# Split products for seven of the eight experts, and the narrowing of a second layer's weights dealt out anew

## The chip, the cores and the metric

The kernel runs on one core of a Trainium2 chip. TensorE is PE here (its weight loads are PEld), VectorE is DVE, ScalarE is ACT, GpSimd is POOL; SP only issues transfers. The metric is the device time of one execution in microseconds, as the median of several runs; less is better.

## The reference, cut to what matters

```python
def reference(...):
    x = attention(q, k, v)            # 2304 tokens of 512 features, unchanged here
    # first layer: 8 experts, 288 tokens each, chosen by a greedy assignment on x @ w_gate
    for e in range(8):
        h = np.maximum(x[assigned == e] @ w1[e], 0.0)      # 512 -> 1024
        out[assigned == e] = h @ w2[e]                     # 1024 -> 512
    # second layer, one weight pair for all tokens
    h = out @ w_in                                         # 512 -> 2048
    sp = np.where(h > 20.0, h, np.log1p(np.exp(np.minimum(h, 20.0))))
    return (h * np.tanh(sp)) @ w_out                       # 2048 -> 512
```

All of it is to be computed to float32 accuracy. The weights `w_in` and `w_out` reach the kernel as 64-bit floats.

## The kernel before, in words

Up to about 205 us the kernel computes the attention and the first routing rounds. Then three things run interleaved:

- **Routing**, one round per expert (`Router.phase`, written R0 to R7). A round picks the next expert and its 288 tokens by a digit search: seven levels, each a comparison on DVE (`cmp`, L353), 18 small counting products on PE (`cnt`, L411), a reduction on DVE (`jk`, L415), a small product (`j`, L417), and two more DVE operations. At its end POOL gathers the token rows (`xrow`, L615), and `r.last` marks the DVE operation that gives their indices.
- **Experts**, E0 to E7 in the order list and one to eight in this text. An expert transposes its rows on PE (`xtp`, L630), copies them to `xh`, and goes through eight slices of 128 hidden features: four products for the hidden slice `hp` (L661), a Relu on ACT (`hh`, L662), and two slices later four products into the output `ya` (L638). All are plain float32 products; PE runs each as two records. The weights come by SP in blocks of 128x512, `w1` from a pool of six buffers and `w2` from one of eight. The output of 288 tokens is split on ACT and DVE into a rounded part `Yh` and a rest `Yl`, which stand in a ring of 512 columns and are stored to `y_dram`.
- **Narrowing**, 32 pieces (`Narrow.steps`): a 128x512 block of 64-bit weights is turned into a rounded float32 and a rest in `wM_sb`. A piece is a load by SP of 0.5 MB into one of two raw buffers, one or two ACT operations, four or five DVE operations with integer bit work, two or three POOL operations and one more on ACT. Its first operation (`hold`) stands behind `r.last`.

The second layer follows in two passes over nine groups of 256 tokens: G for hidden features 0 to 1023, whose results go to `part`, and P for the rest. A group loads `Yh` and `Yl` back from `y_dram` into the ring (POOL's queue, L677), and takes four steps of two slices. A step is 24 split products into `hm` (`mm3`, L597 to L599: rounded by rounded, rounded by rest, rest by rounded, three records of 256 columns each), a chain of five ACT and five DVE operations that gives `gh` and `gl`, and, three steps later, 12 records of 512 columns into `oa`. The G pass needs pieces 0 to 15, the P pass 16 to 31; the latter stand in memory that the experts' pools give back.

The order list says how many pieces follow each expert or group: `E0/2` deals a piece to each of the first two of its eight slices. The order of instructions on each engine is then made by the scheduler of the framework out of this program; every engine takes its instructions strictly in that order.

## Time and profile before

| | |
|---|---|
| median of 2 runs | 1007.25 us (1007.13 to 1007.38) |
| the profiled execution | 1006.99 us, span 1005.2 us |
| PE busy | 918.9 us, 91% of the span, mean clock 0.943 |
| DVE busy | 605.3 us, 60% |
| ACT busy | 435.9 us, 43% |
| POOL busy | 265.2 us, 26% |
| moved by DMA | 123.45 MB, mean 123 GB/s |

The span runs from the first to the last instruction of that execution; the rest of its time lies outside. Busy time of PE is that of records whose ends are modelled, so a full PE says that nothing else was waited for, and the spacing of starts says what one record costs. A bracket behind a timeline row holds the idle time of the engine before it and what ended it. The granted clock is 1.00 at 2.4 GHz and about half at the lower level.

### The profile page before, as it was taken

What the parts mean: (1) busy time and instruction counts of PE and PEld (TensorE: products, weight loads), DVE (VectorE), ACT (ScalarE), POOL (GpSimd) and SP (SyncE); (2) the same over time, 40 slices, a digit from 0 to 9 for tenths busy, and PEclk for the clock granted to TensorE, in tenths of its full rate; (3) what the DMA queues carried; (4) which work ended last, traced back from release to release, by engine and by line L of the source; (5) the groups of instructions that cost most, each with busy time, mean ns of one, the idle gap of its engine ahead of it and who ended that gap; (6) DMA issues with size and microseconds to landing.
All of it is one profiled execution on the core that took longest, in us unless ns stands there. A gap on an engine that the chain in (4) does not pass through costs nothing.

```text
span 1005.2 us, 18188 instructions
## 1 busy us (share of the span) xinstructions
PE 918.9 (91%) x6804; PEld 743.3 (74%) x6804; DVE 605.3 (60%) x1633; ACT 435.9 (43%) x1097; POOL 265.2 (26%) x294
## 2 busy tenths in 40 slices
PE   5999996399999999999977489799999999999995
PEld 3778775267676676767756488688999899999994
DVE  5798885545646454654511599975555565665654
ACT  4577672002121211212321376566565656555553
POOL 5444310204133140406611545530000011111101
PEclk8799997589999999999979689899999999999998
DMA  8557412516455553536741634422222324433311
GB/s 230 150 159 201 145 59 96 150 42 201 133 170 160 166 191 106 191 112 201 252 169 38 160 102 126 126 63 64 64 63 64 84 64 127 111 98 85 84 42 63
DMA packets 76375, 123.45 MB, mean 123 GB/s; under 512 B 12192, under 2 KB 40096, under 8 KB 76288
## 3 DMA queue, kind: packets, MB, share of 16 engines
q1 hardware_dynamic: 36448, 75.10, 24.6%
q0 software_dynamic: 21984, 28.32, 11.1%
q10 hardware_dynamic: 17856, 18.88, 5.5%
q8 instruction: 54, 0.88, 0.4%
q14 instruction: 33, 0.27, 0.1%
HBM read 98.67 MB, written 23.60 MB: 122 GB/s over the span
## 4 chain that ended last, share of the span: by engine, by line
PE 45%; issue 18%; DVE 16%; ACT 10%; POOL 6%; DMA 5%; SPq 0%; POOLq 0%; DVEq 0%; ACTq 0%
PE hp L661 12%; PE ya L638 11%; PE cnt L411 4%; DVE eu L730 3%; DVE eu L729 3%; PE sp L173 3%; PE pvl L213 3%; DVE eu L732 2%; ACT eu L726 2%; ACT r L727 2%; PE trl L199 2%; DMA n<-in_wM_dram 2%; PE rp L229 2%; ACT r L728 2%; DVE gl L736 2%
## 5 line engine op out<-in xcount | busy, mean ns | idle before, releaser
L597 PE MATMUL hm<-Yh,wM_sb 128*128 128x256 f32 x576 | 166.8, 290 | 32.5 <-DMA Yh<-y_dram 16.9
L598 PE MATMUL hm<-Yl,wM_sb 128*128 128x256 f32 x576 | 165.7, 288 | 0.4 <-DMA Yl<-y_dram 0.4
L599 PE MATMUL hm<-Yh,wM_sb 128*128 128x256 f32 x576 | 165.3, 287 | 0.0
L661 PE MATMUL hp<-xh,w 128*128 128x288 f32 x512 | 151.0, 423 | 0.0
L638 PE MATMUL ya<-hh,w 128*128 128x288 f32 x512 | 149.7, 420 | 0.0
L597 PEld LDWEIGHTS hm<-Yh,wM_sb 128*128 128x128 f32 x576 | 113.5, 197 | 39.3 <-DVE eu L732 19.0
L598 PEld LDWEIGHTS hm<-Yl,wM_sb 128*128 128x128 f32 x576 | 114.0, 198 | 3.1 <-DVE nz L551 0.7
L597 PE MATMUL oa<-wM_sb,gh 128*128 128x512 f32 x288 | 113.3, 393 | 2.7 <-ACT gh L735 2.7
L599 PEld LDWEIGHTS hm<-Yh,wM_sb 128*128 128x128 f32 x576 | 113.7, 197 | 0.0
L599 PE MATMUL oa<-wM_sb,gl 128*128 128x512 f32 x288 | 113.6, 394 | 0.0
L598 PE MATMUL oa<-wM_sb,gh 128*128 128x512 f32 x288 | 113.5, 394 | 0.0
L661 PEld LDWEIGHTS hp<-xh,w 128*128 128x128 f32 x512 | 93.2, 192 | 23.5 <-issue 0.2
L729 DVE SCALAR_TENSOR_TENSOR eu<-eu,r 128x512 f32<-128x512 f32 (+1 forms) x73 | 53.4, 731 | 94.2 <-ACT r L728 94.2
L638 PEld LDWEIGHTS ya<-hh,w 128*128 128x128 f32 x512 | 91.6, 190 | 22.7 <-PE hp L661 0.2
L662 ACT ACTIVATE hh<-hp 128x288 f32<-128x288 f32 x64 | 26.0, 408 | 187.0 <-PE hp L661 172.6
L735 ACT CAST gh<-eu 128x512 fp32r<-128x512 f32 (+1 forms) x73 | 44.7, 612 | 107.4 <-DVE eu L732 107.3
L736 DVE TENSOR_TENSOR gl<-eu,gh 128x512 fp32r<-128x512 f32 (+1 forms) x73 | 55.0, 753 | 37.5 <-ACT gh L735 37.4
L726 ACT ACTIVATE eu<-eu,one_sb 128x512 f32<-128x512 f32 (+1 forms) x73 | 52.3, 717 | 42.2 <-DVE eu L725 41.5
L415 DVE TENSOR_SCALAR_CACHE_REDUCE jk<-cnt 8x64 f16<-8x64 f32 (+2 forms) x49 | 11.1, 227 | 92.3 <-PE cnt L411 92.3
L597 PEld LDWEIGHTS oa<-wM_sb,gh 128*128 128x128 f32 x288 | 54.8, 190 | 12.6 <-ACT gh L735 3.2
L599 PEld LDWEIGHTS oa<-wM_sb,gl 128*128 128x128 f32 x288 | 54.4, 189 | 11.8 <-DVE gl L736 0.4
L704 POOL DMA_INDIRECT out_dram<-osb,ixs x18 | 19.4, 1079 | 163.9 <-DVE osb L703 161.1
(151 smaller groups left out, 1697.6 us busy)
## 6 DMA issues: line engine op xcount, KB each, us to landing
w<-in_wE_dram SPq DMA_DIRECT2D x128, 256.0 KB
n<-in_wM_dram SPq DMA_DIRECT2D x32, 512.0 KB
Yh<-y_dram POOLq DMA_DIRECT2D x18, 512.0 KB
Yl<-y_dram POOLq DMA_DIRECT2D x18, 512.0 KB
vw<-in_vw_dram SPq DMA_DIRECT2D x16, 315.0 KB
kT<-in_kT_dram SPq DMA_DIRECT2D x16, 291.0 KB
qT<-in_qT_dram SPq DMA_DIRECT2D x16, 288.0 KB
vd<-in_vd_dram SPq DMA_DIRECT2D x16, 288.0 KB
```

The lines of the kernel that those rows point to most:

```text
L173: self.nc.tensor.matmul(sp[r, u], q[r, 64 * n:64 * n + 64], k[r, 64 * n:64 * n + W], start=False, stop=u == 2)
L213: self.nc.tensor.matmul(op[c, u], vw[:, 3 * g + u, c], d['aT'][:, u, c], start=True, stop=True)
L411: nc.tensor.matmul(cnt[:, 0:K], OH[:, c, :], cmp[c], start=False, stop=(c == 17))
L597: mm(out, lh, rh, start=first, stop=False)
L598: mm(out, lh, rl, start=False, stop=False)
L599: mm(out, ll, rh, start=False, stop=last)
L638: nc.tensor.matmul(acc[c], w2[:, 128 * c:128 * c + 128], hh[:, 0:288], start=j == 0, stop=j == 7)
L661: nc.tensor.matmul(hp, w1[:, 128 * dc:128 * dc + 128], xh[:, dc], start=dc == 0, stop=dc == 3)
L726: nc.scalar.activation(out=u, in_=e, func=AF.Square, bias=one)
L729: nc.vector.scalar_tensor_tensor(out=u, in0=u, scalar=1.0, in1=r, op0=ALU.add, op1=ALU.mult)
L735: nc.scalar.copy(gh[:, 0:w], e)
L736: nc.vector.tensor_tensor(out=gl[:, 0:w], in0=e, in1=gh[:, 0:w].bitcast(F32), op=ALU.subtract)
```

## The change

- Experts two to six (`w` in MODES) keep the plain first product. Their second product becomes a split one: ACT rounds the `w2` block into `wbh` (L607), DVE subtracts for the rest `wbl` (L611), DVE also makes the rest `gl` of the hidden slice (L705), and PE takes three records instead of two per product.
- Experts seven and eight (`s`) split both products. Their weights come as blocks of 128x1024 into three raw buffers; the subtractions go to POOL and DVE in turn; `xh` gets a rest `xl`. Expert one (`p`) stays plain.
- The pools change: for `w1` three buffers instead of six, for the raw `w2` three, for the split weights five and five.
- Narrowing: three pieces in each of experts one to five, one in expert six, none in seven and eight. In the G pass two pieces a group, behind its second and fourth step (`i % 2`) instead of the first two; a piece there may start behind the last `gl` of a step (`mark`) instead of `r.last`. The tile `nt` has one buffer instead of two.
- The ring has 544 columns. Every expert uses columns 256 to 543, the groups 0 to 255 and 256 to 511 in turn.

```diff
@@ -490,10 +490,13 @@
         self.out[k] = idx, exi, ii
-RING = 512
+RING, EPOS = 544, 256
 NV = 3
 LASTM = 1
-NRW, NWA, NWB, NGS = 2, 6, 8, 4
+
+MODES = 'pwwwwwss'
+PE4 = 2
+NRW, NWR, NWA, NWB, NGS = 2, 3, 3, 5, 4
 HC = 8
 LAGE, LAGM = 2, 3
 EXP20 = 485165195.40979
@@ -540,7 +543,7 @@
...
-            t = self.zp.tile([128, 512], F32, name="nt")
+            t = self.zp.tile([128, 512], F32, name="nt", bufs=1)
...
@@ -585,12 +588,28 @@
...
+        self.nsplit = 0
+        self.pooln = PE4
+        self.rawe = P("f_rawe", NWR, ctx_e)
...
         self.wb = P("f_wb", NWB, ctx_e)
...
+        self.mark = None
...
+
+    def split(self, src, pool, nm, eng=None):
+
+        nc = self.nc
+        wh = pool.tile([128, 512], F32R, name=nm + "h")
+        wl = pool.tile([128, 512], F32R, name=nm + "l")
+        nc.scalar.copy(wh, src)
+        if eng is None:
+            eng = nc.gpsimd if self.nsplit % self.pooln != self.pooln - 1 else nc.vector
+            self.nsplit += 1
+        eng.tensor_tensor(out=wl, in0=src, in1=wh.bitcast(F32), op=ALU.subtract)
+        return wh, wl
...
@@ -622,45 +641,69 @@
...
+        mode = MODES[k]
+        plain = mode != 's'
...
-        xh = self.xs.tile([128, 4, 288], F32, name="xh")
+        xh = self.xs.tile([128, 4, 288], F32 if plain else F32R, name="xh", tag="xh")
+        if not plain:
+            xl = self.xs.tile([128, 4, 288], F32R, name="xl")
...
-            (nc.vector.tensor_copy if dc % 2 else nc.scalar.copy)(xh[:, dc], t)
+            if plain:
+                (nc.vector.tensor_copy if dc % 2 else nc.scalar.copy)(xh[:, dc], t)
+            else:
+                nc.scalar.copy(xh[:, dc], t)
+                nc.vector.tensor_tensor(out=xl[:, dc], in0=t, in1=xh[:, dc].bitcast(F32), op=ALU.subtract)
...
-        def second(j, w2, hh):
+        def second(j, w2, hh, hl):
...
-                nc.tensor.matmul(acc[c], w2[:, 128 * c:128 * c + 128], hh[:, 0:288], start=j == 0, stop=j == 7)
+                s = slice(128 * c, 128 * c + 128)
+                if mode == 'p':
+                    nc.tensor.matmul(acc[c], w2[:, s], hh[:, 0:288], start=j == 0, stop=j == 7)
+                    continue
+                self.mm3(acc[c], w2[0][:, s], w2[1][:, s], hh[:, 0:288], hl[:, 0:288], j == 0, j == 7)
             if j == 7:
...
+                q = slice(EPOS, EPOS + 288)
                 for c in range(4):
-                    for s0, s1 in pieces:
-                        q = (pos + s0) % RING
-                        nc.scalar.copy(self.Yh[:, c, q:q + s1 - s0], acc[c][:, s0:s1])
-                        nc.vector.tensor_tensor(out=self.Yl[:, c, q:q + s1 - s0], in0=acc[c][:, s0:s1],
-                                                in1=self.Yh[:, c, q:q + s1 - s0].bitcast(F32), op=ALU.subtract)
-                for s0, s1 in pieces:
-                    q = (pos + s0) % RING
-                    for v, y in enumerate((self.Yh, self.Yl)):
-                        nc.scalar.dma_start(self.a['y_dram'][:, v, :, 288 * k + s0:288 * k + s1].bitcast(F32), y[:, :, q:q + s1 - s0].bitcast(F32))
+                    nc.scalar.copy(self.Yh[:, c, q], acc[c])
+                    nc.vector.tensor_tensor(out=self.Yl[:, c, q], in0=acc[c], in1=self.Yh[:, c, q].bitcast(F32), op=ALU.subtract)
+                for v, y in enumerate((self.Yh, self.Yl)):
+                    nc.scalar.dma_start(self.a['y_dram'][:, v, :, 288 * k:288 * k + 288].bitcast(F32), y[:, :, q].bitcast(F32))
...
+            hh = self.gs.tile([128, 512], F32 if mode == 'p' else F32R, name="gh", tag="gh")
+            hl = None
+            if plain:
+                w1 = self.wa.tile([128, 512], F32, name="w1", tag="wah")
+                nc.sync.dma_start(w1, src[:, 0:512])
+                if mode == 'p':
+                    w2 = self.wb.tile([128, 512], F32, name="w2", tag=("wbh", "wbl")[j % 2])
+                    nc.sync.dma_start(w2, src[:, 512:1024])
+                else:
+                    raw = self.wa.tile([128, 512], F32, name="w2r", tag="wal")
+                    nc.sync.dma_start(raw, src[:, 512:1024])
+                    w2 = self.split(raw, self.wb, "wb", nc.vector)
+                for dc in range(4):
+                    nc.tensor.matmul(hp, w1[:, 128 * dc:128 * dc + 128], xh[:, dc], start=dc == 0, stop=dc == 3)
+            else:
+                raw = self.rawe.tile([128, 1024], F32, name="wraw")
+                nc.sync.dma_start(raw, src)
+                w1 = self.split(raw[:, 0:512], self.wa, "wa")
+                w2 = self.split(raw[:, 512:1024], self.wb, "wb")
+                for dc in range(4):
+                    s = slice(128 * dc, 128 * dc + 128)
+                    self.mm3(hp, w1[0][:, s], w1[1][:, s], xh[:, dc], xl[:, dc], dc == 0, dc == 3)
             nc.scalar.activation(out=hh[:, 0:288], in_=hp, func=AF.Relu)
-            self.push(lambda j=j, w2=w2, hh=hh: second(j, w2, hh))
+            if mode != 'p':
+                hl = self.gs.tile([128, 512], F32R, name="gl")
+                nc.vector.scalar_tensor_tensor(out=hl[:, 0:288], in0=hp, scalar=0.0, in1=hh[:, 0:288].bitcast(F32), op0=ALU.max, op1=ALU.subtract)
+            self.push(lambda j=j, w2=w2, hh=hh, hl=hl: second(j, w2, hh, hl))
...
     def group(self, t0, half):
@@ -670,7 +713,7 @@
...
-        q = 128 * t0 % RING
+        q = 128 * t0 % 512
...
@@ -733,14 +776,14 @@
...
-            nc.vector.tensor_tensor(out=gl[:, 0:w], in0=e, in1=gh[:, 0:w].bitcast(F32), op=ALU.subtract)
+            self.mark = nc.vector.tensor_tensor(out=gl[:, 0:w], in0=e, in1=gh[:, 0:w].bitcast(F32), op=ALU.subtract)
             self.push(lambda f=f, m=m, gh=gh, gl=gl: second(f, m, gh, gl))
...
-ORDER = ('R0 R1 E0/2 R2 E1/2 R3 E2/2 R4 E3/2 R5 E4/2 R6 E5/2 R7 E6/2 E7/2 N G/2 G/2 G/2 G/2 G/2 G/2 G/2 G/2 G P P P P P P P P P').split()
+ORDER = ('R0 R1 E0/3 R2 E1/3 R3 E2/3 R4 E3/3 R5 E4/3 R6 E5/1 R7 E6 E7 N G G G G G G G G G P P P P P P P P P').split()
...
@@ -801,7 +844,7 @@
         nar.st = f.raw
         def hold(ins):
-            tc.add_manual_dep(ins.ins, r.last.ins.name, mybir.DependencyInfo(mybir.DependencyClass.NoSync, mybir.DependencyReason.DATA), reason="order")
+            tc.add_manual_dep(ins.ins, (f.mark or r.last).ins.name, mybir.DependencyInfo(mybir.DependencyClass.NoSync, mybir.DependencyReason.DATA), reason="order")
...
@@ -835,7 +878,7 @@
...
             for i, _ in enumerate(steps):
-                if i < pieces:
+                if i < pieces or i % 2 and st[0] == 'G':
                     nar.piece()
...
```

DVE, from the end of expert two's round to the second level of the next routing round (`nz` and `nt` are a piece's tiles, `jk`, `jb`, `E` and `cmp` the routing's). Before:

```order
L556 SCALAR_TENSOR_TENSOR nt<-n_4214,nt 128x512
L559 TENSOR_SCALAR nz<-nt 128x512
L564 SCALAR_TENSOR_TENSOR nz<-n_4214,nz 128x512
L415 TENSOR_SCALAR jk,fl<-cnt 8x128
L419 TENSOR_REDUCE jb<-j_4379 128x1
L631 COPY xh<-xtp 128x288
L424 TENSOR_SCALAR E<-G,jb 128x36
L631 COPY xh<-xtp 128x288
L353 TENSOR_TENSOR cmp<-E,rthr 128x2304
L405 SCALAR_TENSOR_TENSOR G<-E,dg_4334 128x18
```

In the change:

```order
L557 TENSOR_SCALAR nt<-nz 128x512
L559 SCALAR_TENSOR_TENSOR nt<-n_4242,nt 128x512
L611 TENSOR_TENSOR wbl<-w2r,wbh 128x512
L562 TENSOR_SCALAR nz<-nt 128x512
L705 SCALAR_TENSOR_TENSOR gl<-hp,gh 128x288
L554 TENSOR_SCALAR nz<-nz 128x512
L415 TENSOR_SCALAR jk,fl<-cnt 8x128
L419 TENSOR_REDUCE jb<-j_4506 128x1
L655 COPY xh<-xtp 128x288
L424 TENSOR_SCALAR E<-G,jb 128x36
L557 TENSOR_SCALAR nt<-nz 128x512
L353 TENSOR_TENSOR cmp<-E,rthr 128x2304
```

The round's first level met DVE behind two whole pieces; now a piece is still under way, with a weight split and a rest `gl` between, and the first bit operation of a third piece (L557) stands ahead of the comparison L353.

ACT, at the change from expert seven to expert eight. Before:

```order
L662 ACTIVATE hh<-hp 128x288
L631 COPY xh<-xtp 128x288 x2
L662 ACTIVATE hh<-hp 128x288
L545 ACTIVATE nz<-n_6685 128x512
L545 ACTIVATE nz<-n_6733 128x512
L662 ACTIVATE hh<-hp 128x288
```

In the change:

```order
L702 ACTIVATE gh<-hp 128x288
L607 CAST wbh<-wraw 128x512
L657 CAST xh<-xtp 128x288 x4
L607 CAST wah<-wraw 128x512
L702 ACTIVATE gh<-hp 128x288
L607 CAST wbh<-wraw 128x512
L607 CAST wah<-wraw 128x512
```

The openings of two pieces (L545) stood between the Relus; now copies that round the weights stand there, and the four copies of `xh` are all ACT's.

POOL, where the first group of the G pass loads its input. Before, behind expert eight's pieces:

```order
L562 TENSOR_TENSOR nz<-n_7109,nz 128x512
L567 TENSOR_TENSOR nt<-nt,nz 128x512
L562 TENSOR_TENSOR nz<-n_7162,nz 128x512
L567 TENSOR_TENSOR nt<-nt,nz 128x512
L570 TENSOR_TENSOR wM_sb<-nt,wM_sb 128x512
L677 DMA Yh<-y_dram 128x4x256
L677 DMA Yl<-y_dram 128x4x256
```

In the change, behind expert one's pieces and ahead of the next round of the routing (L456):

```order
L570 TENSOR_TENSOR nt<-nt,nz 128x512
L573 TENSOR_TENSOR wM_sb<-nt,wM_sb 128x512
L720 DMA Yh<-y_dram 128x4x256
L720 DMA Yl<-y_dram 128x4x256
L456 TENSOR_TENSOR si<-sel,rsmall 128x18
L459 TENSOR_TENSOR s_4093<-si,g_4082 128x18
L460 TENSOR_TENSOR R<-si,s_4093 128x18
```

The loads of the first group have moved from the end of the experts to the beginning of the second one.

## Rows read from the trace of the kernel before

**Rows 1.** busy us by stretches (start:end, length, five engines, PEclk, DMA share, GB/s)
```profile
332.10:376.70 44.60, 44.60 (x319) 30.78 (x318) 23.59 (x94) 9.20 (x21) 11.37 (x13) 1.00 0.50 165
466.80:500.70 33.90, 33.67 (x171) 25.93 (x172) 19.31 (x47) 12.49 (x30) 19.31 (x19) 1.00 0.70 229
500.70:511.70 11.00, 2.94 (x15) 2.18 (x14) 4.79 (x7) 2.76 (x6) 4.08 (x4) 0.65 0.59 191
...
547.50:562.20 14.70, 0.09 (x2) 0.07 (x1) 6.03 (x13) 3.89 (x9) 7.28 (x8) 0.64 1.00 256
...
575.00:650.00 75.00, 61.66 (x357) 55.83 (x358) 72.25 (x94) 46.71 (x80) 41.61 (x31) 0.89 0.42 113
675.00:700.00 25.00, 25.00 (x165) 22.79 (x165) 13.71 (x23) 16.19 (x27) 1.48 (x2) 1.00 0.25 64
```

**Rows 2.** PE timeline in expert seven (start, length, line, operation, count)
```profile
475.46 2.10 PE L638 MATMUL ya<-hh,w 128*128 128x288 f32 x8
477.40 2.10 PE L661 MATMUL hp<-xh,w 128*128 128x288 f32 x8
```

**Rows 3.** timeline of PE in the first pass, at clock 1.00
```profile
568.95 0.28 PE L597 MATMUL hm<-Yh,wM_sb 128*128 128x256 f32 x1
569.06 0.28 PE L598 MATMUL hm<-Yl,wM_sb 128*128 128x256 f32 x1
```

**Rows 4.** timeline of ACT: first stores of groups two to five
```profile
644.77 0.58 ACT L699 ACTIVATE osb<-oa 128x512 f32<-128x512 f32 x1
...
670.66 0.58 ACT L699 ACTIVATE osb<-oa 128x512 f32<-128x512 f32 x1
...
691.83 0.59 ACT L699 ACTIVATE osb<-oa 128x512 f32<-128x512 f32 x1
...
713.73 0.59 ACT L699 ACTIVATE osb<-oa 128x512 f32<-128x512 f32 x1
```

**Rows 5.** timeline of PE between experts seven and eight ([idle before <-releaser])
```profile
505.69 0.74 PE L630 MATMUL xtp<-ident_sb,xrow 96*128 96x96 f32 x3 [4.30 <-ACT hh L662]
510.18 0.74 PE L630 MATMUL xtp<-ident_sb,xrow 96*128 96x96 f32 x3 [3.75 <-ACT xh L631]
...
511.73 3.33 PE L661 MATMUL hp<-xh,w 128*128 128x288 f32 x8
```

**Rows 6.** timeline of ACT at the same place
```profile
504.68 0.66 ACT L545 ACTIVATE nz<-n 128x512 f32<-128x512 f32 x1 [5.75 <-DMA n<-in_wM_dram]
```

**Rows 7.** DVE groups of 575:650, 700:1000, 242.7:421.4 (xcount | busy, mean ns, idle)
```profile
L736 DVE TENSOR_TENSOR gl<-eu,gh 128x512 fp32r<-128x512 f32 x10 | 10.9, 1094 | 1.4 <-ACT gh L735 1.4
...
L732 DVE SCALAR_TENSOR_TENSOR eu<-eu,hm 128x512 f32<-128x512 f32 x10 | 6.8, 676 | 0.1
...
L736 DVE TENSOR_TENSOR gl<-eu,gh 128x512 fp32r<-128x512 f32 (+1 forms) x54 | 36.9, 683 | 31.5 <-ACT gh L735 31.5
...
L646 DVE TENSOR_TENSOR Yl<-ya,Yh 128x288 fp32r<-128x288 f32 x8 | 3.6, 455 | 0.1
```

**Rows 8.** POOL groups of 575:650, then its timeline near 286
```profile
L567 POOL TENSOR_TENSOR nt<-nt,nz 128x512 f32<-128x512 f32 x10 | 15.3, 1532 | 19.3 <-DVE nz L564 18.9
L570 POOL TENSOR_TENSOR wM_sb<-nt,wM_sb 128x512 fp32r<-128x512 f32 x9 | 12.6, 1413 | 3.7 <-ACT wM_sb L569 3.7
...
286.33 1.27 POOL L570 TENSOR_TENSOR wM_sb<-nt,wM_sb 128x512 fp32r<-128x512 f32 x1 [0.73 <-ACT wM_sb L569]
```

**Rows 9.** timeline of PE at the first pass, and a row of the waits
```profile
562.16 0.98 PE L597 MATMUL hm<-Yh,wM_sb 128*128 128x256 f32 x3 [14.61 <-DMA Yh<-y_dram]
...
580.90 0.58 PE L597 MATMUL hm<-Yh,wM_sb 128*128 128x256 f32 x1 [6.51 <-DVE eu L732]
...
PEld hm L597 <- ACT wM_sb L569: 15.0, 1, 15.0
```

**Rows 10.** timeline of DVE, first and last of two pieces in an expert
```profile
275.42 0.41 DVE L551 TENSOR_SCALAR nz<-nz 128x512 f32<-128x512 f32 x1
...
279.06 2.19 DVE L564 SCALAR_TENSOR_TENSOR nz<-n,nz 128x512 f32<-128x512 uint32 x1
```

9 lines of the change are left out of this document (removed).

## The prediction

> **What bounds the kernel now.** I read the busy table by stretches first, cut at the places where the work on PE changes [rows 1]. While experts two to six run with a routing round inside (four stretches of 44.6 to 44.7 us, of which one is shown, and a fifth like them), PE is busy in every microsecond at clock 1.00, DVE in 23.6. So PE decides there, and DVE idles for about 21 us. Expert seven (466.8 to 500.7) is as dense. Three places are not: 11.0 us before expert eight, where PE does 2.94; 14.7 us ahead of the first pass, where it does 0.09; and 575 to 650, where PE does 61.66 of 75 while DVE does 72.25. From 675 on PE is full again and DVE has 13.71 of 25. So three different limits: PE among the experts, waits at two seams, DVE at the head of the first pass.
>
> **The products.** The PE timeline shows groups of four plain products, eight records, 1.94 us apart [rows 2]: 0.486 us for one of 288 columns. A split product is three records. The trace has none of 288 columns, but split records of 256 columns start 0.11 to 0.12 us apart [rows 3]. The first store of a group's output comes every 21.9 us (691.83, 713.73) [rows 4]; a group of the pass has 96 records of 256 columns and 48 of 512, so those of 512 cost (21.9 - 96 x 0.12) / 48 = 0.216 us. That bounds a split product of 288 between 3 x 0.12 = 0.36 and 3 x 0.216 = 0.65; 288 lies an eighth of the way, 3 x 0.132, and I take 0.40. The saving is 0.086 us each: 5 experts x 32 second products = 160, 13.8 us; 2 experts x 64 = 128, 11.0 us. At the bounds the 288 products give 36 us or lose 47; the near bound decides, since 32 columns of 256 divide them.
>
> **The seam before expert eight.** PE waits 4.30 us on ACT's Relu, then 3.75 us on ACT's copy of xh [rows 5]. ACT itself stood at the narrowing's Abs until the piece's raw block had landed, 5.75 us [rows 6], and everything behind it in ACT's order waited. In the change pieces stop after expert six's one, so no such instruction stands there (the order rows of ACT). Of the 11.0 us stay 12 transposes of about 0.11 us, 1.3 us; I keep another 1.0 us for PE between transposes and the two-step xh, xl copy. Gain 8.7, and 1.5 more because the granted clock, 0.65 over the stall [rows 1], came back from its lower level of 1.2 GHz only behind it: the eight records there took 3.33 us [rows 5] instead of 2.10 [rows 2]. Together 10.2 us. It could be 4 us less if the extra copies for xl are not covered by second products still queued.
>
> What the split costs the other engines in these two experts: a slice of 128 features is 8 products, 3.2 us of PE. For it ACT makes two rounding copies, DVE or POOL one subtraction each, DVE another for the hidden half. A 128x512 subtraction costs DVE 0.683 us alone [rows 7], one from PSUM over 288 columns 0.455 us, a POOL operation 1.3 us [rows 8]. That is 1.2 us on DVE and 1.3 on POOL beside 3.2 of PE: covered. Raw loads are 0.5 MB per 3.2 us, 164 GB/s; the stretch 466.8 to 500.7 ran at 229 [rows 1].
>
> **The seam before the first pass, and its DVE-bound head.** PE starts the pass at 562.16 after 14.61 us on the load of Yh, and its weight load had 15.0 us of waiting for the last piece of the first half [rows 9]; both end together, so removing one alone brings nothing. The change removes both: the group's columns 0 to 255 are no longer the experts' (now 256 to 543), so the load stands right behind expert one's pieces in POOL's order, and the first half's sixteenth piece is done early in expert seven. Then the pass runs into a 6.51 us wait for DVE [rows 9] and the crowded stretch. All of that together I take from the stores: the third group's first store is at 670.66 [rows 4], and from there the 21.9 us rhythm holds. With PE dense from 547.5 it would come after 7 steps of the first product (168 x 0.12 = 20.2 us) and 3.5 of the second (42 x 0.216 = 9.1), plus two groups: 547.5 + 29.3 + 43.8 = 620.6. So 50.1 us are lost today.
>
> How much comes back hangs on DVE, as 16 pieces remain for this pass. A DVE operation caught by one of POOL takes about a microsecond longer: the subtraction of L736 has a mean of 1094 ns in the crowded stretch, 683 alone [rows 7]. A group without pieces needs DVE for 13.71 x 21.9 / 25 = 12.0 us [rows 1]. Two pieces ran on DVE from 275.42 to 279.06 without their last multiplication [rows 10], so one is 1.82, and about 2.0 with its share of that (0.68 for every third). From 575 to 650 about ten pieces and 10.6 steps of 3.0 us went through DVE [rows 7, 8]: 20 + 31.8 = 52 of its 72.25 us; the other 20 us over POOL's 10 + 9 operations [rows 8] and some 6 multiplications more (POOL's in two of three pieces) is 0.8 each. I price each at 0.8 to 1.0. With two pieces a group: 12.0 + 4.0 + 5.3 x 1.0 = 21.3 at most, under 21.9 by a hair. So the pass should run on PE, with losses: 1 us at its first steps (the last expert's eight copies are ahead on ACT and DVE), 2.5 for the second group, whose columns are the experts' and whose load must wait for the last stores, and 0.5 for each of eight groups. 50.1 - 7.5 = 42.6 us.
>
> [...] If every POOL operation really blocked the routing for its length, the time would be that of rival 2 below; if the blocked time fell where DVE idles, as today, that of rival 1.
>
> **What the plain-and-split experts pay.** Here the change puts work on DVE that PE waits for. An expert gets 8 subtractions x 0.68 = 5.5 us, 8 of 0.455 = 3.6, and a third piece, 2.0. POOL has 8 operations for three pieces instead of 5.3. Today they mostly run while DVE idles in the expert's tail; the order rows of DVE show the third piece reaching into the next routing round, ahead of its comparison. At 0.8 to 1.0 each that is up to 8 us. 23.6 + 5.5 + 3.6 + 2.0 + 7 = 41.7 us of DVE, beside 44.65 - 2.75 = 41.9 of PE: no room left, and the round trips PE, DVE, PE inside a routing level are dead time for DVE. Worse, the tile nt has one buffer: the third piece's shift waits until POOL, ACT and POOL have finished the second, which takes 1.27 + 0.73 + 1.27 = 3.3 us [rows 8], and the routing's comparison, with PE's counting behind it, queues behind that shift. I charge one such chain to each of experts two to six, 5 x 3.3 = 16.5 us. Bounds: nothing (PE has products to fill in) and 5 x (3.3 + 8) = 56 us. The ACT copies (0.62 each) fit into ACT's 35 idle us of 44.6 [rows 1].
>
> **Sum.** 1005.2 - 13.8 - 11.0 - 10.2 - 42.6 + 16.5 = 944.1 us of span. The profiled execution took 1006.99, 1.8 more than its span, and the median is 0.26 above that: 946.2 us. I say 946.
>
> **Rivals.**
> 1. The experts' stalls are filled: PE's order holds products between the counts, and DVE's wait falls beside them. Then only the first three terms count: 946 - 16.5 = 930. For it: DVE idles for 21 us per round today. Against: 41.7 of 41.9.
> 2. DVE decides among the experts: every POOL operation costs the routing its full microsecond on top of half a chain, 5 x (8 + 1.7) = 48 us instead of 16.5: 978. By the port rule of the Trainium skill (SBUF — State Buffer, Who interferes with whom) it would be so wherever POOL starts first. Against it: L353's comparisons and POOL's pieces meet only in the first levels of a round.
> 3. The first pass stays bound by DVE: groups of 25.9 us like the third today (644.77 to 670.66), 4.0 over the rhythm, for eight groups is 32 us instead of the 4 I kept: 974.
> 4. The other side. The third piece's load stands in SP's order ahead of the next weights; it waits for the first piece's raw block to be free. With three buffers instead of six and eight, a weight block then lands late, ACT's copy of it holds DVE's subtraction, and that the routing behind it. One late landing cost ACT 5.75 us [rows 6]. The change loses once experts two to six each lose more than (13.8 + 11.0 + 10.2 + 42.6) / 5 = 15.5 us, three such landings an expert: at four, 5 x 23 - 77.6 gives 1044 us. Against it: bytes per expert grow only by a piece of 0.5 MB, and the stretch ran at 165 GB/s where 229 was reached.
>
> **How the numbers follow.** I give my forecast 0.52, rival 1 0.17, rival 2 0.14, rival 3 0.10, rival 4 0.03; 0.04 stays for a partial failure near the old time. The range 925 to 980 takes in rival 1 with a little of the product's lower bound, and rivals 2 and 3. Faster by over 2% (below 987; about what a measurement of this kernel can tell from no change) gets 0.91, within 2% 0.05, slower 0.04.
>
> **What would show it.** Right: the pass's first product starts within 2 us of expert eight's last; its groups' stores come 22 to 23 us apart from the first on; expert seven and eight take about 59 us together; the period of experts two to six is 44 to 46 us with DVE over 38. Wrong: a period near 42 (rival 1) or over 49 (rival 2), stores 25 us apart (rival 3), ACT's rounding copy of w2 with waits on a DMA of several us (rival 4).

## The result, and the profile after

The changed kernel takes 994.83 us (992.36 and 997.29), a ratio of 0.987 to the kernel before, 95% interval 0.982 to 0.992. 946 had been forecast, 925 to 980. The profiled execution has a span of 995.4 us. Three marks split it: the first transposes of an expert, the end of expert eight's last product, and the first store of a group.

| stretch | before | after | change | forecast |
|---|---|---|---|---|
| up to expert two | 243.9 | 241.3 | -2.6 | 0 |
| experts two to six | 222.0 | 248.0 | +26.0 | -13.8 + 16.5 = +2.7 |
| experts seven and eight | 81.7 | 63.0 | -18.7 | -21.2 |
| from there to the end | 457.7 | 443.2 | -14.4 | -42.6 |

The last row is nearly all in the first pass: from expert eight's end to the eighth group's first store, 231.9 us before and 219.5 after. Before, 14.6 of the 231.9 were the wait ahead of the pass [rows 9]; without it that pass took 217.3. So on balance the change took that wait away and gained nothing else there. Two terms of the sum failed, then, and each alone would have left a good gain.

The busy table by stretches (as [rows 1]: stretch, its length, busy time and instructions of PE, PEld, DVE, ACT and POOL, PE's granted clock, DMA share, GB/s). First experts two to six as a whole, before and after:

```profile
243.90:465.90 222.00, 222.00 (x1574) 152.99 (x1574) 118.46 (x466) 43.16 (x104) 60.27 (x67) 1.00 0.49 156
...
241.30:489.20 247.90, 225.76 (x1725) 170.97 (x1724) 178.96 (x556) 72.38 (x149) 88.92 (x82) 0.93 0.50 160
```

PE was busy for all of the 222.0 us at clock 1.00. Now it is busy for 225.76 of 247.90 at 0.93, which is 225.76 x 0.93 = 210 us of work at the full clock. So its work did fall, by 12 of the 13.8 us; 22 us of waiting and some 16 us at the lower clock came instead.

After the change, expert three, expert seven, expert eight with the head of the pass, and two pieces of 25 us of the pass:

```profile
293.30:342.60 49.30, 45.19 (x352) 34.87 (x351) 34.52 (x115) 15.41 (x32) 16.20 (x16) 0.93 0.47 151
489.20:523.50 34.30, 32.19 (x256) 31.09 (x257) 21.14 (x43) 17.77 (x40) 17.35 (x19) 0.95 0.64 202
523.50:558.00 34.50, 34.50 (x266) 34.30 (x266) 13.46 (x26) 13.95 (x32) 6.49 (x5) 1.00 0.36 116
605.00:630.00 25.00, 22.47 (x139) 19.90 (x138) 18.14 (x27) 15.50 (x26) 10.28 (x8) 0.97 0.38 106
705.00:730.00 25.00, 20.65 (x128) 18.45 (x129) 18.04 (x28) 15.54 (x27) 8.52 (x7) 0.95 0.39 108
```

The seam is closed: PE has no idle time from 523.50 to 558.00. But in the other four stretches no engine is full. Expert three takes 49.3 us with 45.19 of PE and 34.52 of DVE, the pass has gaps on PE with DVE at 18 of 25.

PE's timeline at the seam (start, us, engine, line, operation, output and inputs):

```profile
551.50 0.30 PE L618 MATMUL ya<-gh,wbl 128*128 128x288 f32 x1
551.64 0.29 PE L616 MATMUL ya<-gh,wbh 128*128 128x288 f32 x1
551.77 0.30 PE L617 MATMUL ya<-gl,wbh 128*128 128x288 f32 x1
551.90 0.29 PE L618 MATMUL ya<-gh,wbl 128*128 128x288 f32 x1
552.04 0.28 PE L616 MATMUL hm<-Yh,wM_sb 128*128 128x256 f32 x1
```

Split records of 288 columns start 0.133 us apart, 0.40 a product as estimated from [rows 3], and the pass's first product follows the experts' last at once. ACT's first store of a group, as [rows 4]:

```profile
668.71 0.58 ACT L742 ACTIVATE osb<-oa 128x512 f32<-128x512 f32 x1
...
694.08 0.57 ACT L742 ACTIVATE osb<-oa 128x512 f32<-128x512 f32 x1
...
716.56 0.58 ACT L742 ACTIVATE osb<-oa 128x512 f32<-128x512 f32 x1
...
747.25 0.58 ACT L742 ACTIVATE osb<-oa 128x512 f32<-128x512 f32 x1
...
771.67 0.57 ACT L742 ACTIVATE osb<-oa 128x512 f32<-128x512 f32 x1
```

The intervals are 25.4, 22.5, 30.7 and 24.4 us; the mean over the first eight groups (588.16 to 771.67) is 26.2. Before, the crowd was at the head and 21.9 ruled behind it. The waits from 243 to 489 us (engine, line, what it waited for: us in total, times, longest):

```profile
ACT wbh L607 <- DMA w2r<-in_wE_dram: 66.5, 22, 5.2
...
DVE wbl L611 <- ACT wbh L607: 12.8, 11, 3.4
PE j L417 <- DVE jk L415: 12.2, 5, 5.0
DVE nt L557 <- POOL wM_sb L573: 11.6, 7, 3.2
...
PE xtp L653 <- DMA xrow<-x_dram,idx: 6.4, 4, 2.0
```

PE waits for the routing's level on DVE (jk) and for the rows that the routing gathers. The single nt, to which I had given all of the loss, is 11.6 us on DVE. It stands ahead of the two longest of PE's five waits on jk, 4.99 and 3.06 us; the first of them, DVE and then PE:

```profile
244.56 0.43 DVE L557 TENSOR_SCALAR nt<-nz 128x512 int32<-128x512 int32 x1 [3.15 <-POOL wM_sb L573]
...
246.90 0.18 PE L417 MATMUL j<-reye,fl 8*128 8x8 f16 x1 [4.99 <-DVE jk L415]
```

The waits of up to 5.2 us on w2's load, named as the sign of rival 4, are there too, in front of DVE's subtraction; it stands ahead of the next two of PE's waits, 2.28 and 1.35 us.

### The profile page after: what moved, and what is told of

It is laid out like the page before. It is cut to its first block, busy times and chain, and to the rows that moved or that the text cites. A ratio compares the mean times of both kernels' runs of the same rounds, so it can differ in the third digit from the quotient of the medians.

```text
span 995.4 us, 18889 instructions
## 1 busy us (share of the span) xinstructions
PE 908.2 (91%) x7092; PEld 756.3 (76%) x7092; DVE 667.0 (67%) x1733; ACT 472.4 (47%) x1157; POOL 296.3 (30%) x310
## 4 chain that ended last, share of the span: by engine, by line
PE 52%; DVE 17%; ACT 11%; issue 7%; DMA 6%; POOL 6%; SPq 0%; POOLq 0%; DVEq 0%; ACTq 0%
PE hp L693 8%; PE cnt L411 3%; DVE eu L772 3%; PE ya L616 3%; DVE eu L773 3%; PE pvl L213 3%; ACT eu L769 2%; PE sp L173 2%; PE hm L618 2%; PE hm L616 2%; PE hm L617 2%; PE ya L618 2%; DMA w2r<-in_wE_dram 2%; PE ya L617 2%; ACT r L770 2%
## 5 line engine op out<-in xcount | busy, mean ns | idle before, releaser
L616 PEld LDWEIGHTS hm<-Yh,wM_sb 128*128 128x128 f32 x576 | 110.0, 191 | 27.2 <-DVE eu L775 25.3
L693 PE MATMUL hp<-xh,w 128*128 128x288 f32 x384 | 125.9, 451 | 0.0
L617 PEld LDWEIGHTS hm<-Yl,wM_sb 128*128 128x128 f32 x576 | 110.2, 191 | 1.8
L618 PEld LDWEIGHTS hm<-Yh,wM_sb 128*128 128x128 f32 x576 | 110.0, 191 | 0.0
L772 DVE SCALAR_TENSOR_TENSOR eu<-eu,r 128x512 f32<-128x512 f32 (+1 forms) x73 | 51.3, 702 | 81.1 <-ACT r L771 81.0
L778 ACT CAST gh<-eu 128x512 fp32r<-128x512 f32 (+1 forms) x73 | 44.7, 613 | 101.1 <-DVE eu L775 101.0
L779 DVE TENSOR_TENSOR gl<-eu,gh 128x512 fp32r<-128x512 f32 (+1 forms) x73 | 57.4, 786 | 42.7 <-ACT gh L778 42.5
L693 PEld LDWEIGHTS hp<-xh,w 128*128 128x128 f32 x384 | 71.3, 205 | 15.1 <-issue 0.2
L616 PE MATMUL ya<-gh,wbh 128*128 128x288 f32 x224 | 75.8, 339 | 0.0
L702 ACT ACTIVATE gh<-hp 128x288 fp32r<-128x288 f32 (+1 forms) x64 | 26.2, 409 | 94.3 <-PE hp L693 78.0
L617 PE MATMUL ya<-gl,wbh 128*128 128x288 f32 x224 | 69.7, 311 | 0.0
L618 PE MATMUL ya<-gh,wbl 128*128 128x288 f32 x224 | 68.3, 305 | 0.0
```

Of the source, the lines that this page charges most:

```text
L616: mm(out, lh, rh, start=first, stop=False)
L617: mm(out, lh, rl, start=False, stop=False)
L618: mm(out, ll, rh, start=False, stop=last)
L693: nc.tensor.matmul(hp, w1[:, 128 * dc:128 * dc + 128], xh[:, dc], start=dc == 0, stop=dc == 3)
L702: nc.scalar.activation(out=hh[:, 0:288], in_=hp, func=AF.Relu)
L772: nc.vector.scalar_tensor_tensor(out=u, in0=u, scalar=1.0, in1=r, op0=ALU.add, op1=ALU.mult)
```

## The experiments

The stretches of every run in one table: experts two to six; seven and eight; from expert eight's last product to the eighth group's first store ("pass"). They are of the profiled execution; the time is the median of the runs. Five kernels with the same code for experts two to six gave 243.4 to 248.0 for them, so differences under 5 us there say little; the pass repeats within 0.3 us where its code is the same.

| run | experts 2-6 | 7, 8 | pass | time | ratio to before (95%) |
|---|---|---|---|---|---|
| before | 222.0 | 81.7 | 231.9 | 1007.3 | |
| changed | 248.0 | 63.0 | 219.5 | 994.8 | 0.987 (0.982-0.992) |
| e1_plain | 254.6 | 61.7 | 219.4 | 1000.2 | 0.992 (0.988-0.995) |
| e2_pass_round_only | 243.6 | 62.8 | 188.0 | 965.3 | 0.959 (0.954-0.963) |
| e3_expert_round_only | 234.5 | 61.5 | 219.4 | 983.2 | 0.975 (0.970-0.981) |
| e4_head | 245.8 | 62.4 | 217.6 | 991.2 | 0.983 (0.978-0.987) |
| e5_no_nt_chain | 251.9 | 62.9 | 227.9 | 1007.6 | 0.998 (0.994-1.002) |
| e7_cast_pool | 258.6 | 64.3 | 228.2 | 1011.8 | 1.005 (1.002-1.008) |
| e8_plain_free | 245.1 | 62.9 | 228.0 | 999.5 | 0.992 (0.988-0.995) |
| e9_fewer_second | 215.7 | 71.2 | 232.2 | 986.4 | 0.979 (0.974-0.984) |
| e11_two_pieces | 238.1 | 68.7 | 219.5 | 993.5 | 0.986 (0.981-0.991) |
| e12_two_pieces_split | 242.5 | 73.3 | 219.5 | 999.7 | 0.990 (0.985-0.995) |
| e13_three_eu | 233.9 | 62.2 | 219.5 | 981.7 | 0.973 (0.969-0.977) |
| e14_pass_no_pool | 243.4 | 63.3 | 192.9 | 964.4 | 0.954 (0.947-0.960) |
| e15_quarters | 259.3 | 62.3 | 233.2 | 1019.5 | 1.011 (1.005-1.017) |
| e16_single_raw | 237.6 | 62.1 | 223.3 | 990.3 | 0.984 (0.979-0.989) |
| e17_round_alone | 223.4 | 70.3 | 232.1 | 993.6 | 0.983 (0.977-0.989) |
| e18_pass_dve | 243.8 | 63.1 | 190.8 | 964.3 | 0.957 (0.953-0.962) |
| e19_plain_two_dve | 231.6 | 82.3 | 190.7 | 967.5 | 0.959 (0.956-0.962) |
| e20_plain_three_dve | 242.3 | 61.0 | 190.8 | 964.2 | 0.957 (0.953-0.961) |

### The first pass: do its pieces hold it up, and with what?

**Pieces of the pass only rounded.** In place of a piece's seven steps, while the pass runs:

```diff
+rt = self.st.tile([128, 1024], F32, name="n64", tag="wraw")
+nc.sync.dma_start(rt, self.a['wE'][i // 8, i % 8])
+self.hold(nc.scalar.copy(self.place(i), rt))
```

> Each of the 16 pieces of the first pass is loaded from another block of the same size and rounded by one ACT copy; the narrowing on ACT, DVE and POOL is left out there, so the second half's weights are not the model's. Theory 1 (the pieces hold up the steps of the pass): stores of the groups come 21.9 to 22.5 us apart instead of 22.5 to 30.7 and the first one comes about 5 us earlier, 994.8 - 30 to 38 = 957 to 965 us. Theory 2 (the pass is slow for another reason: the load of a group's columns, or PE's clock): intervals stay near 25 us and the time over 985.

The stores come 22.1 to 22.4 us apart from the second group on, and the pass takes 188.0 us. So the 16 pieces cost 31.5 us, 2.0 each. My sum had the pass come down by 42.6 from 231.9, to 189.3: what it reaches with the pieces as good as gone.

**Pieces at the head of each group, as before.**

```diff
-                if i < pieces or i % 2 and st[0] == 'G':
+                if i < pieces:
```

with `G/2` for eight groups in ORDER and the order held to `r.last`.

> The pieces of the first pass stand behind steps one and two of each group and wait for nothing but the end of the routing, as in the kernel before; the rest is as changed. Theory 1 (each piece costs the pass a fixed amount wherever it stands): the head is crowded as before, three groups at 26 us or more, later ones at 21.9, and the sum over the pass is within 6 us of the changed kernel's, 989 to 1001 us. Theory 2 (spreading itself costs, as a piece then sits inside every second step): the pieces run ahead and cost 15 to 20 us in all, 975 to 985 us.

217.6 against 219.5: the pieces cost 29.6 us crowded and 31.5 spread. Where they stand makes almost no difference, and the spreading is neither gain nor fault.

**Single suspects.** First nt: the sum is built in the raw block, and nt is free again after two DVE operations. Then also the rounding copy:

```diff
-            nc.scalar.copy(h, b['t'])
+            nc.gpsimd.tensor_copy(h, t)
```

> The changed kernel, but the narrowing's sum is built in the raw block's place, so that nt is only used by DVE and free again two instructions later; the same operations otherwise. DVE's wait at L557 for POOL (11.6 us over 7 in the changed kernel, 29.5 over 9 in the run with plain products) goes. Theory 2 (the third piece's chain through the one nt is what holds experts two to six, my 16.5 us): the experts come to about 235 us together instead of 248, 979 to 985 us in all. Theory 1 (DVE's own work of split and pieces): less than 4 us gained, 991 to 996 us.

> As the run without the nt chain, and the rounding copy of a piece moves from ACT to POOL, so that no ACT instruction stands behind POOL's sum. If ACT's wait at L572 (65.9 us over 29 in the changed kernel) is what stretches the steps of the pass, the stores of the groups come 22 to 24 us apart and the pass gives back 15 to 25 of its 30 us: 960 to 975 us. If each piece costs the pass DVE's own time (16 pieces x 1.9 us = 30), the intervals stay near 26 us and the time within 5 us of the run without the nt chain.

The first misses both its figures, the second comes out as its last sentence says; the pass gets longer by 8 us each time. The edits bring a price of their own: the raw block is now held until POOL's subtraction, and ACT's wait for the next block's load rises from 0.3 us over the pass to 13.6 and 26.4. So these two runs do not clear nt or ACT's wait behind POOL's sum; they show only that removing them in this way is of no use.

**Three buffers for eu and r.**

```diff
-            eu = self.mi.tile([128, 2, 512], F32, name="eu")
+            eu = self.mi.tile([128, 2, 512], F32, name="eu", bufs=3)
```

(r likewise, NRW 1, NZ 1.)

> The changed kernel with three buffers instead of two for eu and r, the tiles of a step's activation in the pass; to make room, one raw block and one nz instead of two for the narrowing. If a step's chain is too long for two steps in flight, the stores of the groups come 22 to 23.5 us apart instead of 22.5 to 30.7, 20 us less in the pass (the experts may lose some by the single raw block). If the fixed order on DVE and ACT adds every operation of a piece to a loop that is already as long as a step, the intervals keep their mean of 26.

The second: the pass stays at 219.5 to a tenth. But the single raw block and nz cost something by themselves: with them alone (e16, below) the pass takes 223.3. Beside that, the third buffers are worth 3.8 us, a small part of the 31.5. The larger gain of this run is among the experts (below).

**POOL's part left out.** POOL's operations and the last multiplication are dropped in the pass, ACT rounds both halves.

> The pieces of the pass keep their loads, their ACT operations and four of their DVE operations, but POOL's operations and the last multiplication are left out (ACT rounds both halves instead), so the second half's weights are not the model's. If POOL is at fault (the port that it shares with DVE: 0.69 us become 1.67 to 1.78 in single cases; ACT waiting for POOL's sum), the intervals fall to 22.3 to 23.5 us and 20 us or more come back, about 970 us. If DVE's and ACT's own operations between those of the steps are at fault, they stay at 24.5 to 26 us, 985 to 992 us.

The first expectation: 192.9 us, 26.6 of the 31.5 come back although four DVE operations of each piece and three or four ACT operations stay. It is POOL's part. The timeline of the changed kernel shows what it does, DVE first, then POOL in the same microseconds:

```profile
721.79 0.68 DVE L772 SCALAR_TENSOR_TENSOR eu<-eu,r 128x512 f32<-128x512 f32 x1
722.51 1.69 DVE L773 SCALAR_TENSOR_TENSOR eu<-eu,r 128x512 f32<-128x512 f32 x1
724.12 1.85 DVE L768 TENSOR_SCALAR eu<-eu 128x512 f32<-128x512 f32 x1
...
721.97 1.68 POOL L565 TENSOR_TENSOR nz<-n,nz 128x512 f32<-128x512 f32 x1 [5.56 <-DVE nz L562]
...
724.40 1.27 POOL L570 TENSOR_TENSOR nt<-nt,nz 128x512 f32<-128x512 f32 x1
```

L773 (0.69 alone) ends 0.55 us behind POOL's L565, and L768 (0.42 alone) 0.30 behind L570, although it is recorded as starting 0.28 us ahead of it. Both belong to the step that PE waits for. It is so each time: of a step's DVE operations that took over 1 us in the pass, all 18 with two SBUF inputs (L772, L773, L779) end 0.54 to 0.56 us behind the end of a POOL operation, and all five of L768, which has one, 0.28 to 0.30 us. L775, with one input in PSUM, keeps its 0.68. The Trainium skill (SBUF — State Buffer, Who interferes with whom) has DVE contend with GpSimd also in its two-port modes, which tensor_scalar can enter; L768's rows agree, 0.42 us becoming 1.06 to 1.85.

**POOL's operations in quarters** tests whether this lengthening is the price:

```diff
-            nc.gpsimd.tensor_tensor(out=b['t'], in0=b['t'], in1=b['z'], op=ALU.add)
+            for c in range(0, 512, 128):
+                s = slice(c, c + 128)
+                nc.gpsimd.tensor_tensor(out=b['t'][:, s], in0=b['t'][:, s], in1=b['z'][:, s], op=ALU.add)
```

> The changed kernel with each of POOL's three operations of a piece in four of 128 columns instead of one of 512. If DVE's operations wait for POOL's to end (1.67 to 1.85 us instead of 0.42 to 0.69, 24 us in all over the first pass), each now waits for a quarter at most: the lengthening falls to 6 to 10 us, the pass gives back 12 to 18 us and the experts about 5, 972 to 982 us. If it is POOL's own latency that holds the pieces and the steps behind them, four starts in place of one make it worse: 993 to 1003 us.

Groups of DVE's and POOL's instructions over 220 us of the pass (busy us, mean ns of one | idle before them), changed kernel:

```profile
L779 DVE TENSOR_TENSOR gl<-eu,gh 128x512 fp32r<-128x512 f32 x34 | 30.9, 909 | 18.9 <-ACT gh L778 18.7
L773 DVE SCALAR_TENSOR_TENSOR eu<-eu,r 128x512 f32<-128x512 f32 x34 | 30.3, 891 | 0.7
L772 DVE SCALAR_TENSOR_TENSOR eu<-eu,r 128x512 f32<-128x512 f32 x34 | 24.6, 725 | 22.8 <-ACT r L771 22.8
...
L768 DVE TENSOR_SCALAR eu<-eu 128x512 f32<-128x512 f32 x35 | 21.3, 608 | 8.2 <-ACT eu L767 8.0
...
L570 POOL TENSOR_TENSOR nt<-nt,nz 128x512 f32<-128x512 f32 x16 | 24.8, 1549 | 46.0 <-DVE nz L567 45.2
```

and with quarters:

```profile
L785 DVE TENSOR_TENSOR gl<-eu,gh 128x512 fp32r<-128x512 f32 x32 | 24.9, 780 | 16.9 <-ACT gh L784 16.8
...
L778 DVE SCALAR_TENSOR_TENSOR eu<-eu,r 128x512 f32<-128x512 f32 x32 | 24.4, 763 | 50.0 <-ACT r L777 49.9
L779 DVE SCALAR_TENSOR_TENSOR eu<-eu,r 128x512 f32<-128x512 f32 x32 | 23.1, 723 | 0.6
...
L774 DVE TENSOR_SCALAR eu<-eu 128x512 f32<-128x512 f32 x33 | 15.5, 469 | 10.5 <-ACT eu L773 10.4
...
L574 POOL TENSOR_TENSOR nt<-nt,nz 128x128 f32<-128x128 f32 x60 | 28.7, 507 | 42.2 <-DVE nz L569 42.2
```

Against means of 688, 687, 688 and 429 ns without POOL (run e18), the step's operations (L779 is L736 of [rows 7]) are lengthened by 34 x 0.221 + 34 x 0.204 + 34 x 0.037 + 35 x 0.179 = 22.0 us in the changed kernel, and by 7.8 in quarters. So the lengthening falls as expected, yet the pass is 13.7 us longer, and the time, 1019.5, lies above both figures: POOL now needs 4 x 0.507 = 2.0 us for a sum instead of 1.55, and DVE's idle time behind ACT's r rises from 22.8 to 50.0. The lengthening alone is not the price either; POOL's own latency, passed on through ACT's and DVE's order, is as good a cause.

**A piece without POOL.** Multiplication, sum and subtraction go to DVE in the pass; the line of the sum, one of three:

```diff
-            nc.gpsimd.tensor_tensor(out=b['t'], in0=b['t'], in1=b['z'], op=ALU.add)
+            eng.tensor_tensor(out=b['t'], in0=b['t'], in1=b['z'], op=ALU.add)
```

> The changed kernel with the pieces of the pass entirely on DVE but for ACT's Abs and rounding: multiplication, sum and subtraction move from POOL to DVE, 2.0 us a piece more there, 19.8 of 21.9 us a group. If POOL's lock on DVE is what the pass pays, it takes 195 to 205 us from expert eight to the eighth group's store instead of 219.5: 974 to 984 us. If every DVE operation of a piece adds to the pass, it takes 220 us or more: 995 us and over.

190.8 us, and 964.3 in all, both below the first figure: the whole computation, and 3% less time than the change with one edit more. Its busy rows:

```profile
625.00:650.00 25.00, 25.00 (x158) 22.68 (x157) 22.34 (x41) 17.12 (x30) 2.96 (x4) 1.00 0.43 118
705.00:730.00 25.00, 25.00 (x166) 22.97 (x165) 21.75 (x41) 16.09 (x27) 1.68 (x2) 1.00 0.31 85
```

DVE works 22 of 25 us here and PE never waits; in the changed kernel DVE worked 18 and PE waited 2.5 to 4.4 in such a stretch.

### Experts two to six: what took the place of the saved products?

**Plain again.** `MODES = 'ppppppss'`.

> Experts two to six go back to plain products in both layers; everything else stays as changed (three pieces an expert, single nt, spread pieces, own ring columns). The second products cost PE 13.8 us more. Theory 1 (the split's 16 extra DVE operations an expert overfill DVE beside the routing): the period of experts two to six falls from 46 to 52 us to 44.7 to 46.5, about 994.8 - 25 + 4 = 970 to 975 us. Theory 2 (the third piece and its single-buffered nt hold DVE): the stalls stay and the plain products come on top or fill them: period 48 to 52, 990 to 1008 us.

254.6, and 51 us an expert: theory 2. Without the split the stalls stay. In this run the nt chain does hold; its waits over the experts:

```profile
ACT wM_sb L572 <- POOL nt L570: 41.9, 13, 5.4
...
DVE nt L557 <- POOL wM_sb L573: 29.5, 9, 4.2
```

**Pieces of the experts only rounded** (the edit of e2, for the experts).

> The 16 pieces beside the experts are loaded and rounded by one ACT copy; their narrowing on ACT, DVE and POOL is left out, so the first half's weights are not the model's. The split second product stays. Theory 1a (split alone fills DVE: 23.6 + 9.1 us of operations in the routing's way, without any piece): period stays over 47 us, 985 to 995 us. Theory 1b (split and pieces together overfill DVE and POOL): without the pieces' 3 x 1.8 us of DVE and 8 POOL operations the period falls to 42 to 44 us, 994.8 - 25 to 35 = 960 to 970 us. Theory 2 (the third piece's chain) gives the same as 1b here and parts from it in the run with plain products.

234.5, a period of 47: between the two expectations, and 12.5 over before, though PE has 12 to 14 less to do and no narrowing stands in the way. DVE is not full either, with 136.88 of 234.50 us busy. The four longest of PE's waits on the routing's level, 6.9 us together, all look like this one (ACT, DVE, PE):

```profile
384.44 0.62 ACT L613 CAST wbh<-w2r 128x512 fp32r<-128x512 f32 x1 [3.22 <-DMA w2r<-in_wE_dram]
...
385.09 0.69 DVE L617 TENSOR_TENSOR wbl<-w2r,wbh 128x512 fp32r<-128x512 f32 x1 [3.38 <-ACT wbh L613]
385.70 0.27 DVE L415 TENSOR_SCALAR_CACHE_REDUCE jk<-cnt 8x128 f16<-8x128 f32 x1
...
386.04 0.19 PE L417 MATMUL j<-reye,fl 8*128 8x8 f16 x1 [2.14 <-DVE jk L415]
```

A w2 block lands late, ACT's copy waits for it, DVE's subtraction for the copy, and the routing's reduction stands behind the subtraction in DVE's order. That is rival 4's path and not a full DVE. The load of w2 stands behind that of w1 in SP's order, and SP waits there for a w1 buffer to be given back (from 242 to 477 us; in total, times, longest):

```profile
SPq L690 <- PE hp L699: 96.5, 26, 9.9
```

No run with split products gave w1 more than its three buffers, so that part is read from the trace alone.

**Less work for PE, in the kernel before**, first with its pieces, then with these only rounded:

```diff
-            for c in range(4):
+            for c in range(4 if j in (0, 7) else 2):
```

> The kernel before, with 12 of the 32 second products of each expert left out (half of those of slices two to seven, so the experts' outputs are incomplete): 5.8 us less work for PE per expert. If PE decides among the experts, as I read from its full busy time, the period of experts two to six falls from 44.65 to 38.8 us and the time by 8 x 5.8 = 46.7 to about 962 us. If the routing round's own chain (PE's count, DVE's level, PE's next count) is nearly as long as the period, the period stays at 43 us or more and only the experts without a round gain: 985 to 1000 us.

> The kernel before with the same 12 second products an expert left out as in the run with fewer second products, and the pieces beside the experts loaded and rounded by one ACT copy only (first half's weights not the model's). There the period of experts two to six was 40.0 to 44.5 us with two pieces. If the routing round's chain alone sets that, it stays at 42 us or more. If the two pieces in its way make it so long, it falls to PE's 38.8 to 40.5 us, and experts two to six take 194 to 203 us instead of 216.

29 us less work in experts two to six brought 6.3 us in the one and nothing (223.4) in the other. This is the step that decides the first term. Where it goes, by four microseconds each over the start of an expert in e9:

```profile
364.90:368.90 4.00, 1.63 (x10) 0.99 (x8) 0.35 (x3) 1.02 (x2) 3.41 (x3) 0.82 1.00 337
368.90:372.90 4.00, 4.00 (x14) 2.94 (x15) 2.53 (x6) 0.94 (x2) 0.00 (x0) 0.50 0.22 81
372.90:376.90 4.00, 4.00 (x28) 2.20 (x26) 0.80 (x5) 0.41 (x1) 0.00 (x0) 0.82 0.00 0
376.90:380.90 4.00, 4.00 (x32) 2.53 (x32) 2.11 (x8) 0.41 (x1) 0.00 (x0) 1.00 0.43 137
```

PE arrives early and waits there for the rows, 16.9 us in the five experts of e17, whose PE does 206.86 x 0.94 = 194 us of work at the full clock in 223.3 us:

```profile
PE xtp L636 <- DMA xrow<-x_dram,idx: 16.9, 12, 2.9
...
241.70:465.00 223.30, 206.86 (x1451) 138.26 (x1452) 96.57 (x421) 38.77 (x88) 24.36 (x40) 0.94 0.50 156
```

The next expert's rows are gathered when the routing round is through. The last gather of expert five and the transposes that use it, before and then in e9:

```profile
367.70 0.97 POOL L615 DMA_INDIRECT xrow<-x_dram,idx  x1 [0.30 <-issue]
377.86 0.63 PE L630 MATMUL xtp<-ident_sb,xrow 96*128 96x96 f32 x5
...
360.95 0.97 POOL L615 DMA_INDIRECT xrow<-x_dram,idx  x1 [0.30 <-issue]
367.94 0.74 PE L630 MATMUL xtp<-ident_sb,xrow 96*128 96x96 f32 x3 [0.93 <-DMA xrow<-x_dram,idx]
```

Before, PE reached the transposes 10.2 us behind the gather and had no wait; in e9 the rows land 7.0 us behind it, and PE stands waiting. So some 3 us lay between the two limits here, and they can be gained once: e9's five periods are 40.0, 43.9, 44.4, 44.5 and 42.9 us, against four of 44.7 and one of 43.4 before.

PE waits 2.4 us in that first stretch of four microseconds (1.44 and 0.93), the granted clock falls to 0.50, the 1.2 GHz level, and PE stands as busy while it works at half and then 0.82 of its speed: 2.0 + 0.7 us lost. Wait and lost speed come to 5.1 us of the 5.8 taken away in this expert, whose period is 44.5. So the round, from gather to gather, is the limit right beside PE.

**Plain, without the nt chain; plain with two pieces; split with two pieces; one raw block and one nz.** The edits are those named above, `E0/4 R2 E1/2 ... E5/2 R7 E6/2 E7` in ORDER for the second and third, `NZ = 1` and NRW 1 for the fourth.

> Experts two to six plain in both layers with three pieces each, and both edits of the last run (no nt chain, rounding copy on POOL). If the chain explains the 6.5 us by which the plain period with three pieces (51.1) exceeds the one of before (44.65), the period comes back to 44.7 to 46 us and experts two to six take 224 to 230 us instead of 254.6: 970 to 977 us, less what the pass gains. If the three buffers of the weight ring were the cause, it stays near 51.

> Experts two to six plain in both layers and with two pieces each, as before the change; four pieces in expert one, two in expert six and two in expert seven make up for it. Expert seven and eight split, own ring columns and spread pieces as changed. If the third piece is what takes the plain period from 44.65 to 49 to 51 us, it comes back to 44.6 to 45.5 and experts two to six take 223 to 228 us: 241 + 225 + 63 + 444 + 2 = 975 us, 970 to 980. If the weight ring of three buffers is the cause, the period stays over 48 and the time near 995.

> The same placing of pieces as in the run with two plain pieces, but experts two to six with split second products. With no narrowing at all the split period was 47.0 us, with three pieces 49.6. If the routing round's chain carries the split's 16 DVE operations and each piece's, two pieces give 48 to 49 us, 3 to 4 us over plain: 988 to 995 us. If only the third piece matters, the split pays at last and the period is 42 to 44.6: 965 to 975 us.

> The changed kernel with one raw block and one nz for the narrowing instead of two. If these are what brought experts two to six from 248 to 234 us in the run with three eu (a piece then starts when the one before is through, so that fewer of them meet one level of the routing), it comes back here: 980 to 984 us. If it was the three eu, which the experts do not use, or the placing of tiles, the experts stay at 245 to 250 us and the time at 990 to 996.

e8: 245.1, half-way; the chain was some 9 of e1's 32 us over before, measured with raw blocks that are held longer. e11: periods of 52.0 and 50.3, in which, as I read it, expert one's extra pieces are worked off, then 44.7, 45.9 and 45.2: with two pieces, plain experts are back at their old period, so the weight ring is innocent for plain experts, and the third piece costs about 4 us an expert (e8: 49.0). e12 settles at 47.0 to 47.5: the split costs 2 us an expert there, where it was to save 2.75. e16: 237.6, between its two figures, so most of what e13 gained among the experts is due to the single raw block and nz; e16's pass loses 3.8 of it.

### Both causes together

> Pieces of the pass on DVE; experts two to six plain in both layers with two pieces each as before (three in expert six and seven). If the two causes are all, the parts add up: 241 us to expert two, 223 to 226 for experts two to six (the routing round's chain and plain PE work are both 44 to 45 us), 68 for the last two (three pieces there), 416 from expert eight on, 2 around the span: 949 to 954 us. If the ring of three weight blocks or the single nt still costs, experts two to six stay at 235 us or more: 960 and over.

> Pieces of the pass on DVE; experts two to six plain with three pieces each as changed, one raw block and one nz for the narrowing. A third piece in the round's way costs some 4 us an expert against the run with two; the last two experts are free of pieces (62 us). So 241 + 240 to 245 + 62 + 416 + 2 = 961 to 966 us. If the single raw block keeps the pieces out of the round's way in plain experts too, the experts take 225 to 230 and the time is 946 to 951.

Pass as expected in both. e20 hit its first figure: 242.3 for three pieces, 964.2 us. e19 missed by 15: two plain pieces gave 231.6, and the three pieces in expert seven made the last two experts 82.3 instead of 68. So moving pieces only moves their price. e18, e19 and e20 are equal within their intervals, 4% under before and 3% under the change.

## Why the prediction was wrong

**Right.** The split product (0.40 us), the 24 records of 256 columns in a step (8 split products, not the 24 of the description above), and the closed seam, with the first product 0.14 us after the last one's start. The stall before expert eight is gone (of the 1.5 us that I took for the clock there, the two rows named give 1.2); the two experts take 63.0 where I said 59, since PE has 32.19 of 34.30 busy in expert seven at clock 0.95. Together with the wait ahead of the pass that is 18.7 + 14.6 = 33 us of real gain.

**The first product term, 13.8 us, and the charge of 16.5.** "So PE decides there", read from PE busy in every microsecond [rows 1], was the step that failed, with 16.5 us as the only price of waits. PE's work did fall by 12 us, but 22 us of waiting came instead, and some 16 at the lower granted clock, which the sum had at nothing for these experts. A full engine shows one limit and not the distance to the next. The next, the routing round from gather to gather, lies within 2 us an expert: taking 29 us off PE brought 6 at most. The trace of before has no wait for xrow among these experts; what it has is the 10.2 us from the last gather to the transposes, which I did not set against the time that a gather takes. On top came the new work on ACT and DVE in the round's way: 12.5 us in e3 (no narrowing), where PE's waits on the level are rival 4's path, to which I had given 0.03, and 9 to 13.5 more with the narrowing. Counted against 222.0 - 13.8 it is 39.8 us, between my 16.5 and rival 2's 48. The one nt, my mechanism, is a part of this: DVE waited 11.6 us there, ahead of PE's two longest waits. It is not all, since e3 has no narrowing. Taking the chain away did not help the split kernel (251.9), but that run held its raw blocks longer, so what nt costs by itself is not shown.

**The pass, 42.6 us.** "So the pass should run on PE" compared DVE's busy time, 21.3 at most, with the 21.9 us of a group. DVE's sum was even a little too high (18.1 of 25 us, or 19 a group), and the groups still took 26.2. Rival 3's price, 32 us, is what was measured (31.5), but for another reason than its own: DVE was not full. The pieces' POOL part delayed operations that PE waits for. e18 shows the opposite case, a DVE with 22.3 of 25 and no wait on PE.

**The range.** Rivals 2 and 3 got 0.14 and 0.10 as if one excluded the other. Their prices together, 32 and 28 us on top of 946, make 1006; the result is 995. As I read them, both rest on pieces beside DVE work that PE waits for, so one would most likely bring the other, and the range had to reach there. The signs named for rivals 2, 3 and 4 showed together: a mean period of 49.6, stores 26.2 us apart, waits of 5.2 us on w2.

**Open.** How the pass's 31.5 us divide between POOL's lock on DVE and POOL's latency: each edit that lowered one raised the other. How the 9 to 13.5 us of the narrowing among the experts divide between nt, DVE's operations and POOL's lengthening of them, which no run tested there by itself. Whether w2 would land in time with more buffers for w1. And whether the round would be shorter in e9 and e17 at full clock, since PE's counts are part of it.

## What to carry to other kernels

An engine that is busy all the time is no proof that less work for it saves time: look for the chain that ends at nearly the same moment (here the gather at each expert's start), and try it by leaving out work. Busy time times the granted clock tells what work was done, and so splits a loss into waiting and lost clock. A busy sum below the period is no proof that work fits, either: for work in order on several engines ask whose operation each one delays and who waits for that. Two engines with equal work to share are not always better than one; here moving all of a side job to the fuller engine brought 29 us. And rivals that rest on one cause must be added.
